# Splitting the first transposes over PSUM banks and moving their helper copies to other engines, in a fused linear-attention and squared-ReLU kernel

## Chip, cores, metric

One core of a Trainium2 chip runs the whole program. The metric is the device time of one execution in microseconds (us); lower is better. Times that I read from the trace's records can differ by 0.01 us from those that a view prints.

## The reference, cut to what matters

```python
xn = layernorm(x)                        # x: 2048 tokens x 448, no scale or shift
h  = relu(xn @ w1 + b1) ** 2             # w1: 448 x 1792
g  = silu(h @ w2 + b2)                   # w2: 1792 x 448
s  = linear_attention(xn, wqkv) @ wo     # 16 heads, untouched by the change
out = x + s * g
```

The 448 features are worked on as three chunks of 128 rows and a rest of 64 rows ("rests"). The change touches only the way in: how the first 512 tokens get normalized, transposed and handed to the first matmuls with `w1`.

## The kernel before: the parts that matter

The program is a list of operations, each with what it reads and writes; a small scheduler orders those of ScalarE, DVE (VectorE) and GpSimd by modelled times. TensorE and the queue of loads (SP) run in the order of the list. A token tile has 128 tokens; tiles 0 and 1 are the first pair, tiles 2 and 3 the second. A hidden block is 128 of the 1792 hidden features; `rstd` is the reciprocal standard deviation that the layer norm needs.

The loads are issued in this order, with `w1` in chunks of 512 columns. The 64 rest rows of a chunk are loaded as two pieces into two halves of the partitions:

```python
load_x(0, 1); load_x(1, 2); load_x(2, 4)          # x tiles, on SP
dma("act", b1r ...)                               # the bias, issued by ScalarE
load_w1(0, "sp", "act")                           # first chunk; its rest rows issued by ScalarE
load_w1(1, "sp", "sp")                            # second chunk
load_x(4, 8)
load_k("sp", w_qkv, A_wqkv, "wk", D, 2 * D)
# ... [cut] and later, waiting for the first copy of the second pair:
load_w1(2, "sp", "sp", [("xTp", 2, 0)])           # third chunk
```

The transposes of a pair run on TensorE into PSUM (the memory that TensorE writes its results to, split into banks), and are copied from there to `xT`. For the first pair the three full chunks are one piece of TensorE work; chunks 0 and 2 share a bank. Each tile's rest columns are repeated (`dup`) so that the rests fill 128 rows:

```python
def x_transpose0(lo, between=None):
    bs = [Buf("T"), Buf("T"), None, Buf("T")] if lo == 0 else [Buf("T")] * 4
    bs[2] = bs[0]
    ...  # [cut] piece(cs, tail): two transposes (two tiles) for each chunk in cs
    if lo == 0:
        piece((0, 1, 2), False)      # six transposes, one signal at the end
        piece((3,), True)            # the rests: wait for both dups
    else:
        piece((0, 1, 2, 3), True)    # eight transposes, after both dups
    if lo == 0:
        on_act(0); on_dve(1, 2); on_act(2); between(); return on_act(3)
    on_dve(0, 1); on_dve(1, 2)
    return on_dve(2, 4)

warm(40, 0.107)                      # matmuls on zeros until the first real work
...  # [cut]
x_transpose0(0, lambda: ln_rstd(2, 3))
...  # [cut] norms and dups of tiles 2 and 3
warm(4, 0.056)
for c in range(3):
    pe_part([H0[i] for i in range(4)], 0, (c,))   # 4 hidden blocks: need the first w1 chunk
pe_part([H0[i] for i in range(4, 6)], 0)          # 2 hidden blocks: need the second w1 chunk
t23 = x_transpose0(2)                             # second pair
```

## Time and profile before

| | before |
|---|---|
| time, median of 6 executions (range) | 146.99 us (146.94 to 147.25) |
| span of the profiled execution | 145.4 us |
| TensorE busy | 97% |
| first hidden-layer matmul starts | 6.81 us |
| last matmul starts | 142.26 us |

The page says where to look. Its busy shares, and the chain that ended last:

```profile
PE 141.2 (97%) x1139; PEld 72.3 (50%) x1139; DVE 96.1 (66%) x219; ACT 79.5 (55%) x153; POOL 35.3 (24%) x51
PE 96%; DVE 1%; ACT 1%; issue 0%
```

TensorE is the bound nearly everywhere. In such a kernel an earlier helper gains nothing unless it moves the start of the dense matmul stream or closes a gap in it. The chain in order of time shows the only gaps (start in us, duration in us, what):

```profile
1.06 4.45 PE pb L1089 x40
5.50 0.12 PE pb L784
5.62 0.65 PE pb L741 x6
6.27 0.02 issue
6.29 0.39 ACT xT L761
6.68 0.12 issue
6.81 2.12 PE pb L705 x18
8.93 0.47 PE pb L741 x8
9.40 0.02 issue
9.42 0.30 DVE xT L767
9.72 0.05 issue
9.77 1.48 PE pb L705 x12
14.06 0.76 PE pb L617 x8
14.82 0.86 PE pb L709 x8
```

Between 9.77 and 14.06 lines are left out, all of TensorE. Read it so: 40 warming matmuls (L1089), the bias, six transposes (L741), then the chain leaves TensorE for ScalarE's copy (L761) and comes back at 6.81. After eighteen matmuls and the second pair's eight transposes it leaves once more, for DVE's copy. From 9.77 us on it does not leave TensorE until the last matmul at 142.26 us.

TensorE's waits by releaser agree (waiter, releaser, us in total, times, longest):

```profile
PE pb L1089 <- DVE wz L368: 1.1, 1, 1.1
PE pb L705 <- ACT xT L761: 0.2, 1, 0.2
```

Of the waits of TensorE's weight loads (PEld), one:

```profile
PEld pb L709 <- ACT r L676: 0.2, 1, 0.2
```

One thing this view cannot show: a wait for two things is put down to the one that came last. The first hidden-layer matmul waits for ScalarE's copy and for the load of the first w1 chunk. By the trace's DMA completion records this load landed at 6.67 us (the last of its 16 records); the copy ended at 6.68. "Landing" has this meaning below.

### The profile page before, as it was taken

To read this page: it belongs to the slowest core of one execution; us is meant where nothing else is said; L and a number is where in the kernel's file an instruction comes from. 1 tells how busy PE (TensorE), PEld (TensorE's weight loads), DVE (VectorE), ACT (ScalarE), POOL (GpSimd) and SP (SyncE) were. 2 spreads that over 40 slices of the span, in tenths; PEclk is the share of its full clock that TensorE was granted. 3 is DMA by queue.
4 is the path that set the end of the run, shared out by engine and by line. 5 is a ranking of instruction groups with operands and counts; after the bars stand their busy time and mean duration, and the time that the engine had idled before them with its cause. 6 is when DMAs were issued, how large, how long until landed. Compare 5 with 4: busy or idle time off the path is not lost.

```text
span 145.4 us, 2861 instructions
## 1 busy us (share of the span) xinstructions
PE 141.2 (97%) x1139; PEld 72.3 (50%) x1139; DVE 96.1 (66%) x219; ACT 79.5 (55%) x153; POOL 35.3 (24%) x51
## 2 busy tenths in 40 slices
PE   7999999999999999999999999999999999999992
PEld 7884444444444444444443554454444544544481
DVE  6979888799987995278999500079683516216281
ACT  3627897988886981388879713897311110310300
POOL 2013026470000551630560000000000907306400
PEclk9999999999999999999999999999999999999999
DMA  4967699943301400000000000000000220200312
GB/s 90 316 231 227 146 247 371 330 110 72 77 0 34 111 5 0 0 0 5 0 2 0 5 0 0 0 2 5 0 0 0 66 65 32 95 0 5 126 62 64
DMA packets 16025, 10.53 MB, mean 72 GB/s; under 512 B 7500, under 2 KB 15628, under 8 KB 16012
## 3 DMA queue, kind: packets, MB, share of 16 engines
q1 hardware_dynamic: 15824, 10.28, 25.0%
q8 instruction: 9, 0.15, 0.4%
q10 hardware_dynamic: 188, 0.07, 0.2%
q14 instruction: 4, 0.03, 0.1%
HBM read 6.94 MB, written 1.84 MB: 60 GB/s over the span
## 4 chain that ended last, share of the span: by engine, by line
PE 96%; DVE 1%; ACT 1%; issue 0%
PE pb L970 28%; PE pb L709 26%; PE pb L617 7%; PE pb L797 6%; PE pb L643 6%; PE pb L1039 6%; PE pb L705 3%; PE pb L1089 3%; PE pb L992 2%; PE pb L1075 1%; PE pb L657 1%; PE pb L803 1%; PE pb L874 1%; PE pb L741 1%; PE pb L934 1%; PE pb L826 1%
## 5 line engine op out<-in xcount | busy, mean ns | idle before, releaser
L970 PE MATMUL pb<-w,r 128*128 128x448 bf16 x210 | 41.3, 353 | 0.0
L676 ACT ACTIVATE r<-pb,b1f 128x512 bf16<-128x512 f32 x54 | 33.8, 691 | 10.6 <-PE pb L709 10.6
L709 PE MATMUL pb<-xT,w 64*128 64x512 bf16 (+1 forms) x291 | 38.5, 376 | 0.0
L970 PEld LDWEIGHTS pb<-w,r 128*128 128x128 bf16 x210 | 19.8, 98 | 20.0 <-issue 1.5
L1012 ACT ACTIVATE gbuf<-gbuf 128x448 bf16<-128x448 bf16 x15 | 8.5, 581 | 29.7 <-DVE gbuf L979 29.7
L1028 POOL TENSOR_TENSOR obuf<-obuf,x_tok 128x448 bf16<-128x448 bf16 x12 | 12.0, 1032 | 48.6 <-DVE obuf L1022 48.6
L709 PEld LDWEIGHTS pb<-xT,w 64*128 64x128 bf16 (+1 forms) x291 | 14.1, 94 | 16.6 <-issue 0.4
L627 POOL TENSOR_TENSOR zacc<-zacc,pk 128x448 f32<-128x448 f32 x13 | 14.6, 1126 | 31.4 <-DVE pk L607 28.0
L979 DVE TENSOR_TENSOR gbuf<-pb,b2b 128x448 bf16<-128x448 f32 x15 | 9.4, 623 | 16.5 <-PE pb L970 16.4
L690 DVE TENSOR_TENSOR r<-r 128x512 bf16<-128x512 bf16 x35 | 16.8, 518 | 2.8 <-ACT r L676 2.7
L1022 DVE TENSOR_TENSOR obuf<-pb,gbuf 128x448 bf16<-128x448 f32 (+1 forms) x17 | 9.2, 592 | 6.6 <-PE pb L1039 4.7
L957 DVE TENSOR_TENSOR pqT<-pqT,pb 128x512 bf16<-128x512 bf16 x12 | 7.4, 681 | 8.8 <-PE pb L934 8.8
L617 PE MATMUL pb<-w_qkv,xT 64*128 64x448 bf16 x112 | 13.2, 349 | 0.0
L691 ACT ACTIVATE r<-r 128x512 bf16<-128x512 bf16 x21 | 12.6, 635 | 0.0
L643 PE MATMUL pb<-xT,w_qkv 64*128 64x512 bf16 x84 | 11.0, 376 | 0.0
L709 PE MATMUL pb<-xT,w_1r 64*128 64x512 bf16 x56 | 10.3, 377 | 0.0
L607 DVE SCALAR_TENSOR_TENSOR pk<-pb,pk 128x448 bf16<-128x448 f32 x16 | 9.9, 623 | 0.5
L461 DVE BATCH_NORM_STATS2 st<-x_tok 128x6 f32<-128x448 bf16 x16 | 9.2, 613 | 1.2 <-DMA x_tok<-in_A_x_dram 1.1
L595 ACT ACTIVATE pk<-pb 128x448 bf16<-128x448 f32 x16 | 7.8, 541 | 3.9 <-PE pb L617 3.9
L797 PE MATMUL pb<-pk,xn 128*128 128x448 bf16 x48 | 9.4, 353 | 0.0
L617 PEld LDWEIGHTS pb<-w_qkv,xT 64*128 64x128 bf16 x112 | 5.4, 94 | 6.1 <-issue 0.4
L607 DVE SCALAR_TENSOR_TENSOR pqT<-pb,pqT 128x512 bf16<-128x512 f32 x12 | 8.2, 690 | 0.3
(92 smaller groups left out, 133.7 us busy)
## 6 DMA issues: line engine op xcount, KB each, us to landing
out_dram<-obuf SPq DMA_DIRECT2D x15, 112.0 KB, 1.8
w<-in_B_w_dram SPq DMA_DIRECT2D x1, 1568.0 KB, 9.3
x_tok<-in_A_x_dram SPq DMA_DIRECT2D x3, 448.0 KB, 4.0
w<-in_B_w_dram SPq DMA_DIRECT2D x3, 384.0 KB, 4.5
w_qkv<-in_A_wqkv_dram SPq DMA_DIRECT2D x3, 336.0 KB, 5.7
w_o<-in_A_wo_dram SPq DMA_DIRECT2D x1, 392.0 KB, 9.1
w_qkv<-in_A_wqkv_dram SPq DMA_DIRECT2D x6, 56.0 KB, 5.2
x_tok<-in_A_x_dram SPq DMA_DIRECT2D x2, 112.0 KB, 2.1
```

What stands on the lines that cost most here:

```text
L607: lambda e, _: e.scalar_tensor_tensor(out=slot, in0=ps(buf)[:, 0:n], scalar=1.0 + 1e-6, in1=slot, op0=ALU.add, op1=ALU.max),
L617: return e.matmul(ps(b)[:, 0:D], xT[rw, si, c, :], w_qkv[rw, c, D : 2 * D], start=start, stop=stop)
L627: lambda e, _: e.tensor_tensor(out=o[:, 0:D], in0=pk[:, 0, :] if i == 1 else zacc[:, :], in1=pk[:, i, :], op=ALU.add),
L643: return e.matmul(ps(b)[:, 0:512], w_qkv[rw, c, m * P : (m + 1) * P], xT[rw, 4 * g : 4 * g + 4, c, :], start=start, stop=stop,)
L676: rl = lambda e, _: e.activation(out=slot, in_=ps(b)[:, 0:512], func=AF.Relu, bias=b1f[:, fi : fi + 1])
L690: return e.tensor_tensor(out=slot, in0=slot, in1=slot, op=ALU.mult)
L691: return e.activation(out=slot, in_=slot, func=AF.Square)
L709: return e.matmul(ps(b)[:, 0:512], lhs, xT[rw, 4 * g : 4 * g + 4, c, :], start=start, stop=stop, skip_group_check=not full,)
L797: last = e.matmul(ps(b)[:, 0:D], xn[:, si, c * P : (c + 1) * P], pk[:, si, :], start=(si == 0), stop=(si == NT - 1),)
L970: last = e.matmul(ps(b)[:, 0:D], r2[:, fi, si * P : (si + 1) * P], w_2[:, fi, :], start=(fi == 0), stop=(fi == NF - 1),)
L979: lambda e, _: e.tensor_tensor(out=gbuf[:, si % NGB, :], in0=ps(b)[:, 0:D], in1=b2b[:, :], op=ALU.add),
L1028: lambda e, _: e.tensor_tensor(out=ob, in0=ob, in1=x_tok[:, si, lo:hi], op=ALU.add),
```

## The change

The intent: start the dense stream earlier. Chunk 0 of the first pair is to be copied out as soon as its own two transposes are done, and for this every chunk gets a PSUM bank of its own (the prediction gives the reason). ScalarE copies chunks 0, 1 and 3, DVE chunk 2. The repeats of the rest columns go to GpSimd (DVE keeps tile 3's). In the second pair tile 2 is transposed before tile 3, so that it need not wait for tile 3's repeat. Cut to its core:

```diff
-            if lo == 0:
-                piece((0, 1, 2), False)
-                piece((3,), True)
-            else:
-                piece((0, 1, 2, 3), True)
 ...
-        warm(40, 0.107)
+        warm(36, 0.107)
 ...
-        dup(0, 1)
+        dup(0, 1, "pool")
         ln_rstd(1, 2)
         bias_columns()
+        warm(4, 0.107)
         ln_norm(1)
-        dup(1, 2, True)
+        dup(1, 2, "pool")
         ln_stats(2)
-        x_transpose0(0, lambda: ln_rstd(2, 3))
+        piece, evac = x_transpose0(0, [(0,), (1,), (2,), (3,)])
+        for c in range(4):
+            piece((c,))
+        evac("act", 0, 1)
+        evac("act", 1, 2)
+        ln_rstd(2, 3)
+        evac("dve", 2, 3)
+        evac("act", 3, 4)
 ...
-        dup(2, 3)
+        dup(2, 3, "pool")
         ln_norm(3)
         dup(3, 4)
-        warm(4, 0.056)
 ...
-        t23 = x_transpose0(2)
+        piece, evac = x_transpose0(2, [(0, 1, 2, 3)])
+        piece((0, 1, 2, 3), (0,))
+        piece((0, 1, 2, 3), (1,))
+        evac("dve", 0, 1)
+        evac("dve", 1, 2)
+        t23 = evac("dve", 2, 4)
```

TensorE's later order stays the same. The scheduler, seeing other times, also puts some relus and squares of the first hidden blocks on other engines; in the list above nothing says so.

More of the change, by code (lines that the diff above doesn't have):

```diff
@@ L715, in hh, with dup, x_transpose0, piece @@
             return b, reads + w1names(fi // 4), mm, lambda: h_out(b, g, fi), 512
-        def dup(lo, hi, act=False):
-            if act:
-                add(
-                    "act",
-                    lambda e, _: e.activation(out=xn[:, lo:hi, D:512], in_=xn[:, lo:hi, 384:D], func=AF.Copy),
-                    [("xn", k) for k in range(lo, hi)], [("xnd", k) for k in range(lo, hi)], 0.2,
-                )
-                return
-            add(
-                "dve", lambda e, _: e.tensor_copy(xn[:, lo:hi, D:512], xn[:, lo:hi, 384:D]),
-                [("xn", k) for k in range(lo, hi)], [("xnd", k) for k in range(lo, hi)], 0.12,
-            )
-        def x_transpose0(lo, between=None):
-            bs = [Buf("T"), Buf("T"), None, Buf("T")] if lo == 0 else [Buf("T")] * 4
-            bs[2] = bs[0]
-            def piece(cs, tail):
+        def dup(lo, hi, eng="dve"):
+            add(
+                eng, lambda e, _: e.tensor_copy(xn[:, lo:hi, D:512], xn[:, lo:hi, 384:D]),
+                [("xn", k) for k in range(lo, hi)], [("xnd", k) for k in range(lo, hi)], 0.25 if eng == "pool" else 0.18,
+            )
+        def x_transpose0(lo, pieces, share=()):
+            bs = [None] * 4
+            for p in pieces:
+                b = Buf("T")
+                for c in p:
+                    bs[c] = b
+            for c, o in share:
+                bs[c] = bs[o]
+            def piece(cs, ks=(0, 1)):
                 def f(e, _):
@@ L738, in f @@
                         v = ps(bs[c])[:, :].bitcast(bf)
-                        for k in (0, 1):
+                        for k in ks:
                             o = (c * 2 + k) * P
@@ L744, in piece, with evac, f @@
                 add(
-                    "pe", f, [(("xnd" if tail else "xn"), lo + k) for k in (0, 1)] + ["ident"],
-                    list(dict.fromkeys(bs[c] for c in cs)), len(cs) * 0.114,
-                )
-            if lo == 0:
-                piece((0, 1, 2), False)
-                piece((3,), True)
-            else:
-                piece((0, 1, 2, 3), True)
-            src = lambda c0, c1: (
-                ps(bs[c0])[:, :].bitcast(bf)[:, c0 * 256 : c1 * 256].rearrange("p (c k t) -> p c k t", c=c1 - c0, k=2)
-            )
-            dst = lambda c0, c1: xT[:, lo : lo + 2, c0:c1, :].rearrange("p k c t -> p c k t")
-            def on_act(c):
-                return add(
-                    "act", lambda e, _: e.activation(out=dst(c, c + 1), in_=src(c, c + 1), func=AF.Copy),
-                    [bs[c]], [("xTp", lo, c)], 0.39,
-                )
-            def on_dve(c0, c1):
-                return add(
-                    "dve", lambda e, _: e.tensor_copy(dst(c0, c1), src(c0, c1)), [bs[c0]],
-                    [("xTp", lo, c) for c in range(c0, c1)], 0.1 + 0.16 * (c1 - c0),
-                )
-            if lo == 0:
-                on_act(0)
-                on_dve(1, 2)
-                on_act(2)
-                between()
-                return on_act(3)
-            on_dve(0, 1)
-            on_dve(1, 2)
-            return on_dve(2, 4)
+                    "pe", f, [(("xnd" if 3 in cs else "xn"), lo + k) for k in ks] + ["ident"],
+                    list(dict.fromkeys(bs[c] for c in cs)), len(cs) * len(ks) * 0.057,
+                )
+            def evac(eng, c0, c1):
+                def f(e, _):
+                    src = ps(bs[c0])[:, :].bitcast(bf)[:, c0 * 256 : c1 * 256].rearrange(
+                        "p (c k t) -> p c k t", c=c1 - c0, k=2
+                    )
+                    dst = xT[:, lo : lo + 2, c0:c1, :].rearrange("p k c t -> p c k t")
+                    if eng == "dve":
+                        return e.tensor_copy(dst, src)
+                    return e.activation(out=dst, in_=src, func=AF.Copy)
+                du = 0.37 * (c1 - c0) if eng == "act" else 0.1 + 0.18 * (c1 - c0)
+                return add(eng, f, [bs[c0]], [("xTp", lo, c) for c in range(c0, c1)], du)
+            return piece, evac
         def bias_columns():
```

## The prediction

> **What bounds the kernel now.** The page gives TensorE 97% busy and the chain of waits is 96% TensorE. The time-ordered list of matmuls shows why: from the first real matmul at 6.81 us to the last at 142.3 us they follow one another without a wait but one. Only what moves that start, or a gap after it, changes the time. The view of waits for TensorE has two entries: 1.1 us at the very start, and 0.2 us of the first hidden-layer matmul for ScalarE's copy of the transposed x. The timeline adds a gap of 329 ns in front of 9.77 us where 109 is normal (the second pair's first copy).
>
> **What the change does, costed.** (a) One bank per chunk. Today three chunks' transposes (six, 107 ns apart) end near 6.26 before any copy starts (6.29). The Trainium skill ("PSUM — Partial Sum Buffer", section on bank collisions) says that two engines must not be in one bank at once, hence one bank per early copy. Chunk 0 takes the first two transposes (5.56, 5.64), so its ScalarE copy (384 ns) can start near 5.98 and end near 6.37, not 6.68: 0.3 us earlier. (b) The copy of chunk 1 moves from DVE to ScalarE, chunk 2 from ScalarE to DVE (292 ns): neutral. (c) The repeats of the rest columns (DVE 181 ns, ScalarE 247 ns) go to GpSimd, idle there until 10.3 (237 ns for this shape). (d) Four warming matmuls move ahead of the transposes. (e) Third tile transposed before the fourth, but the first copy of that pair still waits for all eight.
>
> **How much is on the critical path: almost nothing.** The first hidden-layer matmul has two waits: ScalarE's copy and the first w1 chunk. The trace's DMA landings put the last packet of that chunk at 6.67 us; TensorE's semaphore wait for it is recorded at 6.70 for 51 ns, its weight load at 6.78. The copy ended at 6.68: both came together, and the waits view names only the later one. The load is issued at fixed times and does not depend on compute, so the 0.3 us turns into a wait for DMA; I expect the first matmul at 6.76 to 6.81. The 18 matmuls behind it (109 ns each) end at 8.75 as now; the transposes of pair two start at 8.77 now without waiting (its last repeat ended 8.71), so splitting them by tile hides nothing; the gap before 9.77 stays.
>
> The order of relus and squares on ScalarE and DVE changes later, but TensorE's order does not, and DVE loses three 0.18 us copies; I expect no new wait over 0.1 us.
>
> **Prediction:** 146.9 us, 8 in 10 between 146.55 and 147.25. Faster by over 2%: 1%; within 2%: 98%; slower: 1%.
>
> **What would show it.** Chunk 0's copy ends near 6.4; the w1 landing stays at 6.67; the first matmul starts near 6.78, now behind DMA, with TensorE idle about 0.4 us before it; second transposes near 8.75.
>
> **What would make it wrong.** If the load lands earlier in unprofiled runs, up to 0.33 us is gained. If the longer idle time at 6.3 to 6.8 delays the clock (the skill's "TensorE: Matmul & The Clock Gate", "What's actually happening": full clock after a busy window of about 3.4 us; here transposes go from 107 to 56 ns apart at 5.96 us), up to 0.5 us is lost. The reshuffled relus and squares could open a small wait.

## The result, and the profile after

| | before | after |
|---|---|---|
| time, median of 6 executions (range) | 146.99 us (146.94 to 147.25) | 147.05 us (146.73 to 147.26) |
| span of the profiled execution | 145.4 us | 145.4 us |
| first copy ends | 6.68 us | 6.41 us |
| first w1 chunk lands | 6.67 us | 6.36 us |
| first hidden-layer matmul starts | 6.81 us | 6.49 us |
| last matmul starts | 142.26 us | 142.33 us |

The ratio is 0.9999, 95% interval 0.9985 to 1.0014: the same. A ratio here is the mean time of one kernel's fast runs over that of the other's of the same rounds, so it is not quite the ratio of the medians in the table. Executions over 1.5% slower than the fastest of the same kernel are left out of the means.

One profile is one execution: this one took 147.19 us, the second longest of the six (146.73 to 147.26), so it is not said that the others lost the lead in the same way.

The number was predicted. The way to it was not: the stream started 0.32 us earlier, which the prediction had ruled out, and lost it again. The changed kernel's chain in order of time, same columns as above:

```profile
5.74 0.26 PE pb L739 x2
6.00 0.02 issue
6.02 0.39 ACT xT L755
6.41 0.08 issue
6.49 2.30 PE pb L705 x18
8.79 0.46 PE pb L739 x8
9.25 0.02 issue
9.27 0.30 DVE xT L754
9.57 0.05 issue
9.62 1.49 PE pb L705 x12
13.92 0.76 PE pb L617 x8
14.67 0.03 issue
```

Between 9.62 and 13.92 lines are left out again. Only two transposes are left ahead of the copy, as intended. But eighteen matmuls take 2.30 us, not 2.12. And at 14.67 there is an "issue" step in a place where the old kernel had none (14.82 above). Laying the starts of the 1076 real matmuls of both traces side by side gives the lead of the new one, in us; it changes in two places only:

```
matmul      old start   lead of the new kernel
1st            6.81      0.32
13th           8.11      0.15    (two hidden blocks that need the second w1 chunk)
62nd          14.65     -0.05    (hidden blocks that need the third w1 chunk)
last         142.26     -0.07
```

The waits of TensorE's weight loads name releasers for both (same columns as the waits above):

```profile
PEld pb L705 <- DMA w<-in_B_w_dram: 0.3, 1, 0.3
PEld pb L709 <- ACT r L676: 0.4, 1, 0.4
```

The second stood at 0.2 before. The first is a wait for w1 outright: the second chunk landed at 7.92 us and the 13th matmul started at 7.96, where the one before it would have let it start at 7.80. The second line says "a relu on ScalarE". Behind the name stand waits for ScalarE and for three loads. By the trace the last piece of the third chunk's rest rows landed at 14.62, the relu that frees the bank had ended at 14.31, and the matmul started at 14.71 instead of 14.52. So two theories were put to the chip:

- **A: loads.** Each w1 chunk is a gate on the stream, at about 6.4, 7.9 and 14.6 us. An earlier copy helps only where the loads let it, and the loads land when they land.
- **B: the reshuffle.** The lead is lost to relus and squares that the scheduler put elsewhere; the loads are innocent.

### The profile page after: what moved, and what is told of

It is laid out like the page before. It is cut to its first block, busy times and chain, and to the rows that moved or that the text cites. A ratio compares the mean times of both kernels' runs of the same rounds, so it can differ in the third digit from the quotient of the medians.

```text
span 145.4 us, 2854 instructions
## 1 busy us (share of the span) xinstructions
PE 141.3 (97%) x1135; PEld 73.8 (51%) x1135; DVE 93.2 (64%) x216; ACT 79.8 (55%) x153; POOL 35.9 (25%) x54
## 4 chain that ended last, share of the span: by engine, by line
PE 97%; DVE 1%; ACT 1%; issue 0%
PE pb L951 28%; PE pb L709 26%; PE pb L617 7%; PE pb L778 6%; PE pb L643 6%; PE pb L1020 6%; PE pb L705 3%; PE pb L1070 3%; PE pb L973 2%; PE pb L1056 1%; PE pb L657 1%; PE pb L784 1%; PE pb L855 1%; PE pb L915 1%; PE pb L807 1%; PE pb L877 1%
## 5 line engine op out<-in xcount | busy, mean ns | idle before, releaser
L709 PEld LDWEIGHTS pb<-xT,w 64*128 64x128 bf16 (+1 forms) x291 | 15.1, 94 | 15.9 <-ACT r L676 0.4
L627 POOL TENSOR_TENSOR zacc<-zacc,pk 128x448 f32<-128x448 f32 x13 | 14.6, 1120 | 30.7 <-DVE pk L607 30.3
L690 DVE TENSOR_TENSOR r<-r 128x512 bf16<-128x512 bf16 x34 | 14.9, 467 | 3.8 <-ACT r L676 3.6
L691 ACT ACTIVATE r<-r 128x512 bf16<-128x512 bf16 x22 | 13.1, 633 | 0.0
```

Source lines behind the costliest of these rows:

```text
L627: lambda e, _: e.tensor_tensor(out=o[:, 0:D], in0=pk[:, 0, :] if i == 1 else zacc[:, :], in1=pk[:, i, :], op=ALU.add),
L690: return e.tensor_tensor(out=slot, in0=slot, in1=slot, op=ALU.mult)
L691: return e.activation(out=slot, in_=slot, func=AF.Square)
L709: return e.matmul(ps(b)[:, 0:512], lhs, xT[rw, 4 * g : 4 * g + 4, c, :], start=start, stop=stop, skip_group_check=not full,)
```

## The experiments

### Without the w1 gates: `before_free`, `after_free`, `after_free_nosplit`

In both kernels the hidden-layer matmuls of the first 512 tokens read a zeroed tile that has been on chip since 2.4 us. The loads still run and take their share of the queues. The order of instructions on every engine is left as it was, relus and squares included. Their outputs are wrong, which doesn't matter for the times.

```diff
-                if c < 3:
+                if g == 0:
+                    lhs = kvm[rw, c, 0:P]
+                elif c < 3:
                     lhs = w_1[rw, c, fi * P : (fi + 1) * P]
 ...
         pr.schedule()
+        zeros = [o for o in pr.ops if o.writes == ["kvm"]][0]
+        for o in pr.ops:
+            if ...:      # [cut] TensorE, reads w1, first 512 tokens
+                o.deps = {d for d in o.deps if not (d.nbytes and d.writes[0][0] == "w1")} | {zeros}
         pr.emit(nc, es)
```

> The kernel before, but the hidden-layer matmuls of the first 512 tokens read a zeroed on-chip tile instead of w1, so they wait for no w1 load (the loads still run; the result is wrong on purpose; instruction order on every engine unchanged). Theory A (w1 landings absorb the gain): the old kernel is bound at its start by ScalarE's copy at about the same moment as by the load, so it hardly gains: first hidden matmul at 6.75 to 6.81 us, time within 0.1 us of before. Theory B (loads don't matter, the gain is lost to the reshuffled relus and squares): same number. This run is the base line for the next one.

> The changed kernel with the same removal of the w1 waits. Theory A: no stall at the second w1 chunk (8.0 us) nor at the third (14.65 us); the head start of 0.3 us lasts to the end, so the matmul stream at 20 us is 0.25 to 0.4 us ahead of the base line and the time is about 0.3 us (0.2%) below before. Theory B: the stall at 14.65 us is a wait for a relu on ScalarE and stays; the stream is level with the base line from 15 us on and the time equals before.

| | before_free | after_free |
|---|---|---|
| time, median of 6 (range) | 146.97 us (146.90 to 147.92) | 146.85 us (146.65 to 147.22) |
| ratio to before (interval) | 0.999 (0.9959 to 1.002) | 0.9973 (0.9947 to 0.9999) |
| first hidden-layer matmul | 6.59 | 6.44 |
| 62nd matmul | 14.51 | 14.30 |
| last matmul | 142.12 | 141.91 |

Both stalls of the changed kernel are gone. Its chain shows it; the eighteen matmuls take 2.14 us, and the matmuls at 14.46 follow the ones at 13.71 without a break (lines between 6.44 and 13.71 are left out):

```profile
6.00 0.39 ACT xT L757
6.40 0.05 issue
6.44 2.14 PE pb L707 x18
13.71 0.76 PE pb L617 x8
14.46 0.86 PE pb L711 x8
```

The relu order was the same as in the changed kernel, so B falls: the relu named by the waits view did not cost the 0.2 us. The relu is close behind, though: in `after_again` below it ended at 14.24, and the 62nd matmul started at 14.30, just on time. A lead much larger than the one there would meet it. In this very execution the third chunk landed at 14.49, after its matmuls had started, which makes plain that they did not look at it.

The size was off, though. I expected the base line to start at 6.75 to 6.81; it started at 6.59, and the lead was 0.15 us at the start and 0.21 at the end, not 0.25 to 0.4. The step from 0.15 to 0.21 lies at the second transposes: from the 18th matmul to the 19th the base line took 617 ns and the changed kernel 555. The old kernel's own copy had ended at 6.54 in this execution and not at 6.68. The reason is in the trace: TensorE's clock went full at 5.50 us here and at 5.99 in the first profile (the trace's clock record starts there; in the first profile the transposes go from 107 to 56 ns apart at that moment), so the six transposes that the old copy waits for ran faster. The times (0.12 us between the medians) agree in sign, but their intervals do not separate the two.

> As the run before this, but the third and fourth tiles are transposed together again as in the kernel before (one wait for both tiles' rest columns). My prediction said the split hides nothing. Theory A: that holds only while a w1 load delays the 18 matmuls ahead; with the loads out of the way these end near 8.45 us, the fourth tile's repeat ends near 8.55, so undoing the split costs 0.1 to 0.2 us. Rival: the split is worth nothing even then (0.0 us).

```diff
-        piece((0, 1, 2, 3), (0,))
-        piece((0, 1, 2, 3), (1,))
+        piece((0, 1, 2, 3))
```

146.88 us median (146.80 to 147.29), ratio 0.998 (0.9951 to 1.0009). From the 13th to the 19th matmul, with the eight transposes between, it took 1.32 us, against 1.10 us with the split (7.66 to 8.98 and 7.76 to 8.86). The weight loads of the transposes waited for DVE's repeat of tile 3's rests (start, duration, engine, line and operation; in brackets the wait and its releaser):

```profile
8.52 0.45 PEld L741 LDWEIGHTS pb<-ident,xn 128*128 128x128 bf16 x8 [0.33 <-DVE xn L721]
```

With the split there is no such bracket:

```profile
8.31 0.54 PEld L741 LDWEIGHTS pb<-ident,xn 128*128 128x128 bf16 x8
```

So without the split 0.22 us were lost in this execution. But its stream had also started 0.10 us sooner (6.34; its clock had gone full at 4.75 us), while tile 3's repeat ended at the same time in both (8.47 and 8.48). Had the stream of `after_free`, whose first of these transposes started at 8.42, waited for that repeat, I estimate a loss of about 0.1 us. The split is worth 0.1 to 0.2 us once the stream arrives early, as expected. The last matmul started 0.12 us later than in `after_free`; the timed medians (146.88 and 146.85 us) cannot separate the two.

Against the old kernel it was worth less. In four of the old kernel's profiles (`before_again`, `before_free`, `before_early`, `before_merge_late`) the 19th matmul came 617 to 621 ns after the 18th, in the first one 560; in the changed kernel with its split it is 555 or 556. There TensorE's weight load had waited for tile 3's repeat (8.58 after 8.53 in `before_again`). So the split can hide 0.06 us of the old kernel's time, and next to nothing in the one profile that the prediction was made from.

### The landings vary by themselves: `before_again`, `after_again`, `after_more`

Unchanged kernels, again.

> The kernel before, unchanged, for a second look at when the w1 loads land. If landings vary from execution to execution by themselves, the first chunk lands anywhere in 6.3 to 6.7 us, the second in 7.7 to 8.0 and the last of the third chunk in 14.3 to 14.7. If the earlier landing (6.36) of the changed kernel's profile was an effect of the change, this one lands at 6.65 to 6.7 again.

> The changed kernel, unchanged, for a second look at the landings. Theory A: whatever the first landing is, the stream of matmuls after 15 us starts within 0.1 us of the landing of the third chunk's last part; if that lands at 14.6 again, the time is again that of the kernel before.

> The changed kernel, unchanged, once more, for more timed executions and a third profile. From the landings of the first w1 chunk in the ten profiles so far (6.14 to 6.92, mean 6.47 us) and the end of the first copy (6.60 us on average in the old kernel's profiles, 6.34 in the new one's), I work out a mean gain of about 0.1 us: ratio 0.999 to 1.000, not separable from 1. The first hidden matmul starts at the later of copy end + 0.06 and landing + 0.14.

| us | before | before_again | after | after_again | after_more |
|---|---|---|---|---|---|
| first w1 chunk lands | 6.67 | 6.14 | 6.36 | 6.32 | 6.14 |
| second lands | 7.79 | 7.36 | 7.92 | 7.47 | 7.48 |
| last piece of the third | 14.52 | 14.26 | 14.62 | 13.60 | 14.00 |
| last matmul | 142.26 | 142.08 | 142.33 | 141.92 | 142.04 |

The earlier landing of the changed kernel's profile was not an effect of the change: the old kernel's second profile has an even earlier one (6.14). Over all profiles with the same first load the averages are level: 6.42 in four of the old kernel and its variants, 6.45 in seven of the changed one. All three ranges that I had expected for the landings of `before_again` were too narrow (6.14, 7.36 and 14.26). Nor is it the chip alone: the jobs ran on different chips, and within one job the first chunk still landed at 6.14 to 6.61 (four profiles) and at 6.31 to 6.92 (four).

In `after_again` the two later gates were open in time, and the correct kernel kept its whole lead: 0.36 us at the first matmul and 0.35 at the last, against the old kernel's first profile (against `before_again` 0.11 and 0.17). The expectation that the stream would start within 0.1 us of the third chunk's landing did not hold: it landed at 13.60, and the 62nd matmul started at 14.30, because it no longer waited for it. The first gate still held, by 0.09 us. Here the chain itself starts in the load, which a reader of one profile alone would not have guessed:

```profile
2.20 4.12 DMA w<-in_B_w_dram
6.31 0.14 issue
6.45 2.12 PE pb L705 x18
14.46 0.88 PE pb L709 x8
```

`before_again` and `after_again` have one timed execution each (state unknown): 146.96 and 146.79 us. `after_more` had six, median 146.89 us (146.68 to 147.28), ratio 0.9971 (0.9945 to 0.9996), outside the 0.999 to 1.000 that I expected. In that job the old kernel itself was slower than before (median 147.25, up to 148.08), so I do not take the 0.3% at its word. Over all jobs, pooled although they ran on different chips, the old kernel has 40 timed executions, median 147.18, lowest 146.90; the unchanged changed kernel has 13, median 146.92, lowest 146.68. A gain of some 0.2 us is likely; it is not settled, and what lengthens some of the old kernel's executions to 148 us was not found.

Thirteen profiles that are not slow give one rule for the first hidden-layer matmul, to within 0.02 us: it starts at the later of (copy end + 0.06) and (landing + 0.14).

| profile | copy ends | first chunk lands | later of the two sums | start |
|---|---|---|---|---|
| before | 6.68 | 6.67 | 6.81 | 6.81 |
| before_again | 6.50 | 6.14 | 6.56 | 6.55 |
| before_free (no load wait) | 6.54 | - | 6.60 | 6.59 |
| before_early | 6.70 | 6.58 | 6.76 | 6.75 |
| before_merge_late | 6.80 | 5.78 | 6.86 | 6.85 |
| after | 6.41 | 6.36 | 6.50 | 6.49 |
| after_again | 6.30 | 6.32 | 6.46 | 6.45 |
| after_more | 6.38 | 6.14 | 6.44 | 6.43 |
| after_free (no load wait) | 6.39 | - | 6.45 | 6.44 |
| after_free_nosplit (no load wait) | 6.29 | - | 6.35 | 6.34 |
| after_early | 6.26 | 6.92 | 7.06 | 7.06 |
| after_early_split | 6.42 | 6.63 | 6.77 | 6.76 |
| after_merge | 6.44 | 7.08 | 7.22 | 7.21 |

In the eleven profiles with the original loads up to this point the first chunk landed at 6.14 to 6.92 us (in the three without a load wait, at 6.28, 6.16 and 6.61). The old copy ended at 6.60 on average in four of them, the new one at 6.35 in seven. Putting those two averages and the eleven landings through the rule gives a mean start of 6.73 and 6.61 us: an estimate of 0.12 us for the gain at the start, less what the later gates take back.

### Opening the later gates: `after_early`, `before_early`, `after_early_split`

The third chunk's load is issued without its wait for the second pair's first copy. The region it writes is used by nothing earlier; the result is correct.

```diff
         pr.schedule()
+        for o in pr.order["sp"]:
+            if o.writes == [("w1", 2, 0)]:
+                o.deps.clear()
         pr.emit(nc, es)
```

> The changed kernel, correct, with one dependence dropped: the third w1 chunk (and the loads behind it on the queue) is issued without waiting for the first copy of the second pair; instruction order unchanged. Theory A: the stall of 0.2 us in front of 14.7 us goes away and 0.15 to 0.3 us of the head start lasts; time 0.1 to 0.3 us below before (the wait for the second chunk near 8 us stays). Theory B: the stall stays (ScalarE's relu), no gain. What could spoil it: the earlier load takes bandwidth from the x tiles and the k weights.

> The same dropped dependence in the kernel before. Theory A: the old kernel reaches that point at 14.65 us when the load has just landed (14.52), so it gains at most 0.1 us. If it gains as much as the changed kernel does, then the gain is of the load alone and not of the change behind it.

| | after_early | before_early |
|---|---|---|
| time, median of 6 (range) | 146.99 us (146.84 to 147.34) | 146.93 us (146.89 to 147.16) |
| ratio to before (interval) | 0.9982 (0.9957 to 1.0006) | 0.9976 (0.9951 to 1.0001) |
| last piece of the third chunk lands | 12.97 | 12.19 |
| first chunk lands, first matmul | 6.92, 7.06 | 6.58, 6.75 |

The stall in front of the 62nd matmul is gone in the changed kernel, as A expects: its distance to the old kernel's first profile is the same from the first matmul (0.25 us behind) to the last (0.25 us behind). But in this execution the first chunk landed at 6.92, so the stream began late, and the profile shows the other side of the gate: copy ended at 6.26, stream started at 7.06. In times the two are level. Dropping the wait brings no gain that these runs can show, and the changed kernel is not ahead with it: the expected 0.1 to 0.3 us was a miss or lies inside the noise. In this execution the first gate outweighed the third.

> The run before the last, and the second w1 chunk loaded in two halves, so that the two hidden blocks needed at 7.8 us wait for 192 KB fewer. Theory A: the second stall (0.16 us near 8 us) shrinks to under 0.05 us too, and the time is 0.25 to 0.4 us below before: the version that beats both. Risk: one more issue (about 0.65 us) on the load queue delays the next x tiles, which could make a new wait near 10 us.

```diff
+            for i, (l, h) in enumerate([(lo, lo + 256), (lo + 256, hi)] if p == 1 else [(lo, hi)]):
                 dma(
-                    eng, w_1[:, :, lo:hi], B_w1[0:384, lo:hi]...
+                    eng, w_1[:, :, l:h], B_w1[0:384, l:h]...
```

147.91 us median (147.14 to 148.19), ratio 1.0035 (1.0007 to 1.0063): slower, by about 0.4%. The second gate did open (half chunk landed at 7.22, no stall at the 13th matmul). The named risk came true, elsewhere than I had thought. TensorE waited 0.7 us for a relu in front of the 62nd matmul:

```profile
PE pb L710 <- ACT r L677: 0.7, 1, 0.7
```

Here the releaser is real, and DVE's timeline shows what held it up:

```profile
9.37 0.82 DVE L755 COPY xT<-pb 128x256 bf16<-128x256 bf16 x3 [0.70 <-PE pb L740]
11.21 2.21 DVE L462 BATCH_NORM_STATS2 st<-x_tok 128x6 f32<-128x448 bf16 x4 [1.02 <-DMA x_tok<-in_A_x_dram]
13.33 0.36 DVE L464 BATCH_NORM_AGGREGATE mv<-st 128x2 f32<-128x6 f32 x4
```

The x tiles 4 to 7, queued behind one more load, landed 0.9 us later than the old kernel's first profile had them (its statistics start at 10.31); the statistics follow; and in ScalarE's program these tiles' rstd (at 14.05) stands ahead of the relus that free the banks (from 14.17). A load that none of these matmuls waits for had become a gate. How much of the 0.9 us the extra load caused is not shown: it moved the issue of these tiles by 0.5 us (4.78 to 5.30), and of the load's 16 completion records the fifteenth came at 9.94, the last alone at 11.19. In unchanged kernels this load landed at 8.86 to 10.29.

### Fewer and later loads of the rest rows: `after_merge`, `after_merge_late`, `before_merge_late`

One load for a chunk's rest rows instead of two; and in the "late" kernels those of the first chunk are issued after tile 1's rstd instead of first of all. All three are correct.

```diff
-            for i in (0, 1):
-                dma(
-                    eng2, w_1r[64 * i : 64 * i + 64, 256 * p : 256 * p + m],
-                    B_w1[384:448, lo + m * i : lo + m * i + m], [("w1", p, 1 + i)], 128 * m,
-                )
+            src = B_w1[384:448, lo : lo + m]
+            src = bass.AP(tensor=src.tensor, offset=src.offset, ap=[[m, 2]] + list(src.ap))
+            dma(eng2, w_1r[:, 256 * p : 256 * p + m], src, [("w1", p, 1), ("w1", p, 2)], 256 * m)
 ...
-        load_w1(0, "sp", "act")             # the late kernels only
+        load_w1(0, "sp", None)
 ...
         ln_rstd(1, 2)
+        load_w1r(0, "act")
```

> The changed kernel, correct, with the two loads of each w1 chunk's rest rows made into one (same bytes, same queues, three issues fewer on the load queue; compute order unchanged). Theory: the third chunk's last part lands 0.5 us earlier (13.1 to 14.1 instead of 13.6 to 14.8), so no stall in front of 14.65 us; the first landing is unchanged. 0.05 to 0.15 us below the changed kernel.

> As the run before, and the rest rows of the first chunk (64 KB, needed at 11 us) are loaded by ScalarE only after tile 1's rstd (5.0 us) instead of ahead of everything. Theory: the first two w1 chunks land 0.1 to 0.4 us earlier, the first hidden matmul is bound by the copy (6.35 to 6.5 us) and the stream runs without a stall: 0.2 to 0.35 us below before. Risk: the issue on ScalarE (0.6 us) pushes the first copy later, or the rest rows land after 11 us.

> The same two load changes in the kernel before. Theory: the old kernel is then bound by its own first copy (6.5 to 6.7 us, start at 6.56 to 6.75): at most 0.1 us below before, and 0.15 to 0.25 us behind the changed kernel with the same loads. If it is level with that one, the change is worth nothing even with early loads.

| | after_merge | after_merge_late | before_merge_late |
|---|---|---|---|
| time, median of 6 (range) | 147.76 us (147.51 to 149.61) | 149.95 us (148.40 to 151.10) | 148.64 us (148.35 to 151.21) |
| of these fast, and their median | 6, 147.76 us | 4, 149.09 us | 5, 148.56 us |
| ratio to before (interval) | 1.0059 (1.0010 to 1.0108) | 1.0129 (1.0080 to 1.0179) | 1.0088 (1.0057 to 1.0120) |

Six of the eighteen executions, three of them counted as fast, have a mean granted clock of 0.987 to 0.989. In the one of them that was profiled (`after_merge_late`) the clock was at half from 13.93 to 17.34 us, after TensorE had stood 2.09 us for the merged load; whether the wait caused it is not shown. Without its two such executions `after_merge` still has 147.51 to 147.87 us.

All three are misses, and the traces point to one reason. In the changed kernel each half of the first chunk's rest rows has 16 completion records, the last at 3.97 and 5.07 us. The merged load, issued at the same 1.51 us, has three: at 2.56, 5.62 and 6.03. The Trainium skill ("DMA: Bandwidth & Descriptors", section "Why a DMA increments its semaphore by 16 and not by 1") says that the number of DMA engines is the largest up to 16 that divides the slowest dimension of both sides, and that for the engines not used the count is raised at once. The merged source has a slowest dimension of 2: two engines carry the load, and the early record is the fourteen others. The trace agrees with this: two late records and an early one. The load lasted until 6.03 instead of 5.07 us, and the first w1 chunk landed at 7.08 in this profile, so the stream started at 7.21. Of that chunk's own 16 records fourteen had come by 6.05 and two came at 6.86 and 7.07, which fits two engines that were kept busy; no run separates this from the ordinary spread. The third chunk's last part landed at 14.83, not at 13.1 to 14.1.

The idea behind "late" may be right in its first half. With the rest rows out of the way the first chunk landed at 5.78 us in `before_merge_late`, earlier than in any other profile, and the old kernel's stream was bound by its copy (6.80, start at 6.85); but in the (slow) profile of `after_merge_late` it landed at 6.24, inside the usual range. In both the two-engine load came too late. The chain of `before_merge_late` shows it:

```profile
4.80 7.78 DMA w_1r<-in_B_w_dram
12.59 0.05 issue
12.63 0.61 PE pb L708 x4
```

The matmuls that need it had started at 11.18 in the old kernel's first profile; from there on the stream was 1.3 us further behind. The profile of `after_merge_late` is slow and is not compared with the others in time, but it stood at the same place:

```profile
13.31 0.61 PE L708 MATMUL pb<-xT,w_1r 64*128 64x512 bf16 x4 [2.09 <-DMA w_1r<-in_B_w_dram]
```

Whether the late load alone, with its two pieces kept, would have paid is open. Nor do these two runs decide what the change is worth with early loads.

## Why the prediction was right, and where not

- **Time: right, in part by luck.** 146.9 us predicted, 147.05 measured, ratio 0.9999. The stated range (146.55 to 147.25) would have held a gain of the full 0.3 us too, so the time alone does not test the mechanism; and in the profile the lead was taken back by two gates that the prediction did not name.
- **TensorE is the bound, and only its start and its gaps count: right.** In the thirteen traces the lead or lag against the first profile changes by more than 0.03 us from one matmul to the next only at these places: the second and third w1 chunk, the second transposes, the relu of `after_early_split`, the merged rest-row load, and the first two intervals of `after_more`, where the clock was not yet full.
- **The copy is 0.3 us earlier: right.** 6.41 instead of 6.68 in the first pair of profiles; 6.35 instead of 6.60 on average. The mechanism is the one meant: two transposes ahead of the copy instead of six. It also makes the copy less dependent on when the clock goes full: the old copy's end follows that moment in its five profiles (from 6.50 with a full clock at 5.20 to 6.80 at 6.79), the new one's does not (6.38 at 6.75, but 6.44 at 6.02; all between 6.26 and 6.44).
- **"The load is issued at fixed times and does not depend on compute, so the 0.3 us turns into a wait for DMA": this step failed.** From fixed issue times I concluded a fixed landing ("the w1 landing stays at 6.67"). The issue is fixed, the landing is not: 6.14 to 6.92 us over eleven profiles with the same loads up to this point. The prediction did name an earlier landing as what could make it wrong, but as a trait of unprofiled runs. In the profile after it landed at 6.36, and the first matmul started at 6.49 and not at 6.76 to 6.81. The gate was named rightly and taken for a constant. By the estimate above about half of the copy's 0.25 us turns into a wait for this load on average, not all of it.
- **What took the lead back.** Not the first gate but two later ones in that execution: 0.16 us at the second w1 chunk and 0.2 us at the third. Removing the w1 waits removed both; in `after_again`, where the loads happened to come early, the lead over the old kernel's first profile lasted to the end (0.36 and 0.35 us).
- **"Splitting them by tile hides nothing": true of the profile that it was read from, wrong in general.** In the profile after, the second chunk had made the stream late anyway. The old kernel lost 0.06 us there in its four other profiles, and with the w1 waits gone undoing the split costs 0.1 to 0.2 us.
- **"Four warming matmuls move ahead of the transposes": misread.** Four are dropped. That left TensorE idle before the stream, but no later full clock is seen: 4.75 to 6.75 us in the changed kernels, 5.20 to 6.79 in the old ones (slow profile left out).
- **"The gap before 9.77 stays": right.** 329 ns before; after, the matmul at 9.62 follows the one at 9.29 by 331 ns.
- **"No new wait over 0.1 us": wrong,** but not because of the relus and squares: both new waits were for loads.
- **The clock: a real term that I saw only as a risk.** It goes full between 4.75 and 6.79 us in these profiles, in both kernels. In `after_more` it did so only at 6.75, and the first two intervals between matmuls were 188 and 180 ns where 109 is usual: 0.15 us of a lead of 0.38. It moves both kernels and adds to the spread that hides a gain of 0.1 to 0.2 us. The longer idle time did not delay it, as the bullet on the warming matmuls shows.

Open: the exact mean gain (the estimate is 0.12 us at the start; the timed medians differ by 0.36 us in one job and by -0.06 in another), why one load lands 0.8 us apart in different executions, and the occasional executions of 148 us.

## What to carry to other kernels

When two things release an instruction at nearly the same moment, the waits view names one of them; look up when each came before you count on moving one, and look in more than one execution, because a load's landing can move by more than the gain that you are after. A lead won at the front has to pass every later gate, and a load that is just in time today is the next gate. Before you merge small loads, look at how many engines the merged one will use: its completion records tell.

## What the Trainium skill lacked or had wrong

- "DMA: Bandwidth & Descriptors": it gives fixed costs and bandwidths of a load, but I found no spread between executions of one program; here the same 384 KB load, at the same place in the queue, landed at 6.14 to 6.92 us. Its rule for the number of engines was right and would have saved three runs (three completion records instead of 16).
- "TensorE: Matmul & The Clock Gate", section "What's actually happening": it says that the moment of the change to full clock varies by ±500 ns. In these twelve profiles with a clock record (the slow one left out) it came at 4.75 to 6.79 us with matmuls running from 1.06 us in all of them, a spread of 2 us.
- "PSUM — Partial Sum Buffer", section on bank collisions: no run here tested it; the prediction took from it the reason for one bank per chunk, and nothing was found lacking.
